# Output stage of a fused top-k attention and two-MoE kernel: raw loads gated two half steps up and no longer chained, and single tiles for gate, value, rounded and rest parts

## The chip, the cores and the metric

The kernel runs on one core of one Trainium2 chip. The metric is the device time of that core for one execution, in microseconds (us). The engines are TensorE (PE in the profile; PEld is its weight loads), VectorE (DVE), ScalarE (ACT), GpSimd (POOL), and SyncE (SP), which issues most of the DMAs. Each engine works through its own instructions in the order in which the program has them.

## The reference, cut to what matters

```python
x = topk_attention(q, k, v)               # batch 4, 8 heads, 576 tokens, head size 64 -> x: [2304, 512]
g = x @ w_gate                            # first MoE, width 1536
x = (g * sigmoid(g)) * (x @ w_val) @ w_out
h = x @ w_in                              # second MoE, width 2048
out = (h * np.cos(h)) @ w_out2            # [2304, 512]
```

All of it is float32. The kernel multiplies in a rounded format by splitting a number into its rounded part and its rest, and takes three products (rounded by rounded, rest by rounded, rounded by rest).

## The kernel before, in words

The program is not written in the order of its instructions. Generators (`gop_proc`, `half_proc`, `join_proc`, `row_proc` and so on) describe chains of steps; each step names an engine, an assumed cost, a due time and whether it starts only when the step before it has ended (the last field, `dep`). A small planner (`Plan.run`, L131) plays these chains against each other: whenever an engine is free in the plan, the ready step with the earliest due time is emitted. `Ring` counts buffers of a tile, and `gate(k)` holds a chain until buffer use k minus n is released; `Event` holds a chain until something is done. The planner's times decide only the order of the instructions on each engine. On the chip an instruction waits for its data and for its buffer, and for everything ahead of it on its engine.

A DMA step has an assumed cost of 1.2 and a latency of 2.0 in the plan (L96). With `dep` true, a chain's next load is ready only when the load before it has landed in the plan.

There are three stages that matter here.

- The attention and the first MoE. For a chunk of up to 256 tokens and 128 columns of the width, ScalarE copies the gate (tile `th`, tanh, and its copy `hg`) and the value (`vv`) out of PSUM, GpSimd multiplies them, ScalarE writes the rounded part and GpSimd the rest into a tile `g` (L859 to L988). `th` with `hg`, and rounded part with rest, each share one tile of [128, 2, 256].
- The hidden stage (`h_proc`, L1403, products at L1417). It multiplies by `w_in` with seven products for each two-by-two block instead of eight (the matrices are first added up into seven combinations), for 4 column blocks of 576 tokens and 16 pairs of rows: h. `cosine` (L1555) turns h into h cos h with a chain ACT, DVE, ACT, ACT, DVE (L1565, L1573, L1578, L1581, L1582) with 2 buffers `k` and 4 buffers `r`; `row_proc` stores the rows to `gd` in HBM (L1598). Every fourth row of the width is stored without the cosine, but for the first 512 tokens; its cosine is taken late, in the output stage. The turns of `cosine` follow one another in the order of the list `sequence` (L1551).
- The output stage. It has 18 half steps s = 0 to 17 (`HS`, L1614): 9 groups of 256 tokens, each with two halves hh of the width. A half step loads four raw blocks of h cos h from `gd`: A11, A21, A22, A12 (`load`, L1774). VectorE makes four sums of them (S3, S1, S2, S4, L1799). For each of the seven operands in `W_ORDER`, ScalarE writes the rounded part (L1821) and VectorE the rest (L1825) into a tile `gp` with 7 buffers, and TensorE runs 12 matmuls of 128x256 (`product`, L1878). In half steps with hh = 1 of group 2 and later, A22 and A12 go through `cosine` first (`late_proc`). After the second half `join_proc` (L1890) adds the seven results up, 7 VectorE instructions (L1926 to L1944), and stores two rows of output blocks (L1911); their due time puts them ahead of everything else. The weights of the output product are split likewise (`wout2_proc`, L1710 and L1713, 28 tiles), when the hidden stage releases the tiles that they go to. `sums_proc` (L1620, adds at L1657) makes their sums during the hidden stage.

Raw blocks have five buffers for even half steps (the tag `xr`) and five for odd ones (`wr`), so half step s takes the buffers of s-2 (`raw_slot`, L1731). Half step 1 is an exception: its A11 lies in the tile `th` and its A21 and A22 in the two tiles `g`, which the first MoE no longer needs, its A12 in a tile `six`, and S3 in a buffer `r`.

What sets the order of the loads is the head of `gop_proc` and its loop over the loads:

```python
s = step_of[g, hh]
if s:
    yield ev_s3[HS[s - 1]]                 # L1750: S3 of the half step before is made
...
for m, a, b in (("A11", 0, 0), ("A21", 1, 0), ("A22", 1, 1), ("A12", 0, 1)):
    yield ring.gate(i)                     # L1840: the buffer is released
    t = yield "DMA", 1.2, load, due(m) - 8.0, True      # L1841
```

Of the kernel before, what the change touches and what calls it, by code (L numbers as in the profile page):

```python
# [24 lines left out]
DM = H * D  # L25
# [15 lines left out]
CB = S  # L41
# [2 lines left out]
ALONE = 1  # L44
BOTH = 5
LATE = (3,)
GLEAD = 12.0
HALF = S // 2
SCALE = 1.0 / math.sqrt(D)
STEEP = 2.0 ** 96  # L50
# [114 lines left out]
def topk_attention_moe_moe(ctx: ExitStack, tc: tile.TileContext, qT, kT, vP, w1, wo1, w2, out):  # L165
# [667 lines left out]

    G, GT = {}, {}
    r_gv = [Ring(1), Ring(1)]
    r_th, r_vv, r_g, r_yo = Ring(1), Ring(2), Ring(2), Ring(1)
    r_y = [Ring(1) for _ in range(NYB)]
# [17 lines left out]
    TH, VV = {}, {}  # L857

    def wide(tag, n, dt=F32):  # L859
        ring = {"vv": r_vv}.get(tag, r_g)  # L860
        return moe.tile([128, MH], dt, tag=tag, name=tag, bufs=ring.n)[:, :n]

    def gates(n):
        t = moe.tile([128, 2, MH], F32, tag="th", name="th", bufs=r_th.n)
        return [t[:, a, :n] for a in range(2)]

    def gated(dt):
        return moe.tile([128, 2, MH], dt, tag="g", name="g", bufs=r_g.n)

    def gate_proc(k, n, gate, ring, i, due, done):  # L870
        yield r_th.gate(k)

        def evac():
            th, hg = TH[k] = gates(n)
            nc.scalar.activation(th, gate, AF.Tanh, scale=0.5)
            nc.scalar.activation(hg, gate, AF.Copy)  # L876

        end = yield "ACT", 0.13 + 0.00157 * n, evac, due - 10.0, True
        ring.free(i, end, plan)
        done.set(end + plan.LAT["ACT"], plan)  # L880
# [12 lines left out]
    def gemm_proc(c, f):  # L893
        k = K0[c] + f
        due = moe_due(c, f)
        if f:
            yield ev_gemm[c, f - 1]
        yield ev_x[c]
        yield ev_w1[f]
        last = c == NCH - 1  # L900
        if last:
            yield ev_psb
        n = SIZES[c] * 128
        gv, done = {}, [Event(), Event()]

        def part(g, kk):
            xh, xl = XH[c, kk][:, :n], XL[c, kk][:, :n]
            for i, (a, m) in enumerate(((0, xh), (0, xl), (1, xh))):
                nc.tensor.matmul(gv[g], W1[f, kk // 2][:, a, g, kk % 2], m, start=kk == 0 and i == 0,  # L909
                                 stop=kk == KT - 1 and i == 2)  # L910

        rings = []
        for g in range(2):
            if last:
                ring, i = r_o[(2 * f + g) % NLAST], (2 * f + g) // NLAST
                yield ring.gate(i)
                gv[g] = pools["psB"].tile([128, DM], F32, tag=f"o{(2 * f + g) % NLAST}", name="gvl")[:, :n]
            else:
                ring, i = r_gv[g], GV0[c] + f
                yield ring.gate(i)  # L920
                gv[g] = gvt[g][:, :n]
            rings.append((ring, i))
            for kk in range(0, KT, RUN_KK):
                run = range(kk, kk + RUN_KK)
                end = yield ("PE", (0.08 + 0.00117 * n) * RUN_KK,
                             lambda g=g, run=run: [part(g, k2) for k2 in run], due, False)
                if g and f == NF1 - 1:
                    for k2 in run:
                        r_x.free(x_index(c, k2), end, plan)
            if not last:  # L930
                plan.start((gate_proc, val_proc)[g](k, n, gv[g], ring, i, due, done[g]), end + plan.LAT["PE"])
            elif not g:
                plan.start(tanh_proc(k, n, gv[g], due, done[g]), end + plan.LAT["PE"])
        ev_gemm[c, f].set(end, plan)
        if last:
            done[1].set(end + plan.LAT["PE"], plan)
            yield done[0]
            yield done[1]
            yield r_vv.gate(k)
            th = TH.pop(k)  # L940
            if f == NF1 - 1:
                ev_tanh.set(done[0].time, plan)

            def silu():
                VV[k] = wide("vv", n)
                nc.vector.scalar_tensor_tensor(VV[k], th, 1.0, gv[0], op0=OP.add, op1=OP.mult)

            def product():
                nc.vector.scalar_tensor_tensor(VV[k], VV[k], 0.5, gv[1], op0=OP.mult, op1=OP.mult)

            end = yield "DVE", 0.36, silu, due - 80.0, True
            rings[0][0].free(rings[0][1], end, plan)
            r_th.free(k, end, plan)
            end = yield "DVE", 0.36, product, due - 80.0, True
            rings[1][0].free(rings[1][1], end, plan)
            vv = VV[k]
        else:
            for g in range(2):
                yield done[g]
            th, hg, vv = TH.pop(k) + VV.pop(k)  # L960
            mul = 0.05 + 0.0026 * n
            yield ("POOL", 0.05 + 0.00135 * n,
                   lambda: nc.gpsimd.tensor_scalar(th, th, 1.0, 0.5, op0=OP.add, op1=OP.mult), due, True)
            yield "POOL", mul, lambda: nc.gpsimd.tensor_mul(th, th, hg), due, True
            end = yield "POOL", mul, lambda: nc.gpsimd.tensor_mul(vv, th, vv), due, True
            r_th.free(k, end, plan)
        yield r_g.gate(G0[c] + f)

        def hi():
            t = gated(F32R)  # L970
            G[c, f] = [t[:, a, :n] for a in range(2)]
            nc.scalar.activation(G[c, f][0], vv, AF.Copy)

        yield "ACT", 0.07 + 0.00092 * n, hi, due, True
        eng, name, cost = (nc.vector, "DVE", 0.33) if last else (nc.gpsimd, "POOL", 0.05 + 0.0025 * n)
        end = yield name, cost, lambda: eng.tensor_sub(G[c, f][1], vv, G[c, f][0]), due - 80.0 * last, True
        r_vv.free(k, end, plan)
        ev_g[c, f].set(end, plan)

    def tanh_proc(k, n, gate, due, done):  # L980
        yield r_th.gate(k)

        def evac():
            TH[k] = gates(n)[0]
            nc.scalar.activation(TH[k], gate, AF.Tanh, scale=0.5)

        end = yield "ACT", 0.27, evac, due - 10.0, True
# [2 lines left out]
    def turned_gemm_proc(c, fp):  # L990
# [27 lines left out]
        gate, val = bank[:, :, 0], bank[:, :, 1]  # L1018

        def evac():  # L1020
            st["th"], st["hg"] = gates(CH)
            st["vv"] = wide("vv", CH)
            nc.scalar.activation(two("th"), gate, AF.Tanh, scale=0.5)
            nc.scalar.activation(two("hg"), gate, AF.Copy)
            nc.scalar.activation(two("vv"), val, AF.Copy)
# [24 lines left out]
        def fetch():  # L1050
            if stored:
                g = xslot[2 + c].rearrange("p a b -> p (a b)")[:, fp * CH:fp * CH + CH]
            else:
                at = c, (fp - NG0) // 2
                if at not in GT:
                    GT[at] = gated(F32)
                g = GT[at][:, fp % 2]
            G[c, fp] = g.rearrange("p (f n) -> p f n", f=2)
            nc.scalar.activation(G[c, fp], st["ps"], AF.Copy)

# [486 lines left out]
    def width_of(n):  # L1547
        j, f = divmod(n, NF2)
        return CB if f % 4 not in LATE else 0 if j else WIDE

    sequence = [n for n in range(NCB * NF2) if width_of(n)] + ["S3"] + [  # L1551
        (g, hh, a) for g in range(WIDE // 256, NGRP) for hh in range(2) if 2 * hh + 1 in LATE for a in range(2)]
    turn_of = {x: i for i, x in enumerate(sequence)}

# [64 lines left out]

    def sums_proc(q):  # L1620
        hh, w = divmod(q, 2)
        due = b_due(3 + 5 * q)
        tiles = {}
        have = {m: Event() for m in ("B11", "B12", "B21", "B22", "T1", "T2", "T3", "T4")}
        used = {m: Event(n) for m, n in (("B11", 1), ("B12", 2), ("B21", 1), ("B22", 2), ("T1", 2), ("T2", 2),
# [105 lines left out]
    def raw_slot(g, hh, m):  # L1731
# [5 lines left out]
            return pb, "xr", r_xr, 6 * NCB + 5 * (s // 2) + k  # L1737
        if s > 1:
            return pb, "wr", r_wr, W2R + NQ2 * SEVEN + 5 * (s // 2 - 1) + k
        g0 = G0[NCH - 1] + NF1  # L1740
        return {"A11": (moe, "th", r_th, K0[NCH]), "A21": (moe, "g", r_g, g0), "A22": (moe, "g", r_g, g0 + 1),
                "A12": (pools["pbx"], "six", r_six, 0), "S3": (pools["pbx"], "r", r_r2, turn_of["S3"])}[m]

    def members(m):
        return slice(m, NF2, 4)

    def gop_proc(g, hh):
        s = step_of[g, hh]
        if s:
            yield ev_s3[HS[s - 1]]  # L1750
        if s == 3:
            yield ev_wt[NQ2 * SEVEN - 1]
        for j in range(g * 256 // CB, (g * 256 + 255) // CB + 1):
# [4 lines left out]
        used = {m: Event(n) for m, n in (("A11", 3), ("A21", 2), ("A22", 2), ("A12", 1), ("S1", 2), ("S2", 2),  # L1758
                                         ("S3", 1), ("S4", 1))}
        home = {"S1": "A21", "S2": "A11", "S4": "A12"}  # L1760

        def due(m):
            return o_due(s * SEVEN + (W_ORDER.index(m) if m in W_ORDER else 2)) - GLEAD

        def alloc(m):
            pool, tag, ring, _ = raw_slot(g, hh, m)
            shape = {"xr": [128, 2, HN], "r": [128, CB], "th": [128, 2, MH], "g": [128, 2, MH]}.get(tag, [128, DM])
            x = pool.tile(shape, F32, tag=tag, name="gr", bufs=ring.n)
            tiles[m] = (x.rearrange("p a b -> p (a b)") if len(shape) == 3 else x)[:, :DM]

        def load(m, a, b):
# [16 lines left out]
        def add(m, x, y, op, wait=()):  # L1788
# [9 lines left out]
                    tiles[m] = tiles[home[m]]  # L1798
                nc.vector.tensor_tensor(tiles[m], tiles[x], tiles[y], op=op)  # L1799

            t = yield "DVE", 0.62, fn, due(m) - 2.0, True
            have[m].set(t, plan)
            done(x, t)
            done(y, t)
            if m == "S3":
                if "S3" in turn_of and s == 1:
                    r_k2.free(turn_of["S3"], t, plan)
                    ev_rows[turn_of["S3"]].set(t, plan)
                ev_s3[g, hh].set(t, plan)
# [18 lines left out]
            ev_gp[g, n, hh].set(t, plan)  # L1828

        def s3():  # L1830
            _, tag, ring, i = raw_slot(g, hh, "S3")
            if tag == "r":
                yield ev_rows[i - 1]
                yield r_k2.gate(i)
            yield ring.gate(i)
            yield from add("S3", "A11", "A21", OP.subtract)

        for m, a, b in (("A11", 0, 0), ("A21", 1, 0), ("A22", 1, 1), ("A12", 0, 1)):
            _, _, ring, i = raw_slot(g, hh, m)
            yield ring.gate(i)  # L1840
            t = yield "DMA", 1.2, lambda m=m, a=a, b=b: load(m, a, b), due(m) - 8.0, True  # L1841
            if b and (g, hh, a) in turn_of:
                plan.start(late_proc(m, a), t)
            else:
# [192 lines left out]
```

## Time and profile before

| | us |
|---|---|
| median of 3 runs | 1257.4 (1253.33 to 1262.25) |
| profiled execution | 1262.9 |
| its span, first to last instruction | 1260.8 |
| TensorE busy | 1172.8 (93%) |
| VectorE busy | 1104.5 (88%) |
| ScalarE busy | 962.8 (76%) |
| GpSimd busy | 575.0 (46%) |

The span is what the trace shows; the execution has 2.1 us around it. In rows of the trace "idle before" is the time in which an engine did nothing just ahead of an instruction, and the name behind the arrow is what ended last of the things that it waited for. `SPq` is the queue of SyncE. A row with a count merges instructions that follow one another; its time runs to the end of the last.

### The profile page before, as it was taken

To read this page: it belongs to the slowest core of one execution; us is meant where nothing else is said; L and a number is where in the kernel's file an instruction comes from. 1 tells how busy PE (TensorE), PEld (TensorE's weight loads), DVE (VectorE), ACT (ScalarE), POOL (GpSimd) and SP (SyncE) were. 2 spreads that over 40 slices of the span, in tenths; PEclk is the share of its full clock that TensorE was granted. 3 is DMA by queue.
4 is the path that set the end of the run, shared out by engine and by line. 5 is a ranking of instruction groups with operands and counts; after the bars stand their busy time and mean duration, and the time that the engine had idled before them with its cause. 6 is when DMAs were issued, how large, how long until landed. Compare 5 with 4: busy or idle time off the path is not lost. (4 is left out here: it accounts for less than half of the span.)

```text
span 1260.8 us, 25036 instructions
## 1 busy us (share of the span) xinstructions
PE 1172.8 (93%) x8368; PEld 1048.2 (83%) x8368; DVE 1104.5 (88%) x2181; ACT 962.8 (76%) x2152; POOL 575.0 (46%) x1036
## 2 busy tenths in 40 slices
PE   6699889999999999999999999999899997889898
PEld 3476647898879998888888988999899997888787
DVE  7999989999999999998999992759988997767776
ACT  4789989888889898898888975549887994434543
POOL 5898966876688767787766655000000000000000
PEclk9899989999999999999999999999999999989999
DMA  7555556665565645566555442753667775434422
GB/s 252 167 167 166 178 161 187 210 214 157 172 186 165 210 157 168 170 183 203 163 183 180 137 129 82 225 158 112 205 208 253 213 235 155 115 96 126 114 84 67
DMA packets 149488, 211.60 MB, mean 168 GB/s; under 512 B 20592, under 2 KB 96880, under 8 KB 149360
## 3 DMA queue, kind: packets, MB, share of 16 engines
q1 hardware_dynamic: 149200, 209.94, 53.6%
q8 instruction: 66, 1.08, 0.4%
q14 instruction: 62, 0.51, 0.1%
q10 hardware_dynamic: 160, 0.07, 0.0%
HBM read 159.62 MB, written 50.33 MB: 167 GB/s over the span
## 5 line engine op out<-in xcount | busy, mean ns | idle before, releaser
L628 DVE MAX8 m<-w 128x8 f32<-128x576 f32 x432 | 309.6, 748 | 1.8
L909 PE MATMUL gv<-x,w 128*128 128x256 f32 x2016 | 271.2, 286 | 0.5 <-ACT th L876 0.5
L909 PEld LDWEIGHTS gv<-x,w 128*128 128x128 f32 x2016 | 252.1, 190 | 3.1 <-ACT th L876 1.3
L1878 PE MATMUL b<-w2o,gp 128*128 128x256 f32 x1512 | 198.8, 292 | 28.1 <-ACT gp L1821 14.5
L1878 PEld LDWEIGHTS b<-w2o,gp 128*128 128x128 f32 x1512 | 190.5, 197 | 36.2 <-DVE gp L1825 19.0
L631 DVE MATCH_REPLACE8 w<-m,w 128x576 f32<-128x576 f32 x288 | 213.2, 743 | 0.0
L1417 PE MATMUL b<-xc,w 128*128 128x288 f32 x1344 | 184.9, 299 | 6.3 <-DVE h L1483 3.2
L1417 PEld LDWEIGHTS b<-xc,w 128*128 128x128 f32 x1344 | 181.6, 190 | 8.5 <-DVE h L1483 4.1
L1080 PE MATMUL y<-wo,g 128*128 128x512 f32 x608 | 170.8, 415 | 9.8 <-POOL wo L249 3.9
L1080 PEld LDWEIGHTS y<-wo,g 128*128 128x128 f32 x608 | 107.1, 189 | 40.9 <-POOL wo L249 5.9
L1821 ACT ACTIVATE gp<-gr 128x512 fp32r<-128x512 f32 x126 | 73.5, 624 | 81.5 <-DVE gr L1799 58.9
L659 ACT ACTIVATE e<-s,b 128x576 f32<-128x576 f32 x144 | 113.5, 789 | 9.5 <-POOL b L642 9.2
L628 DVE MAX8 m<-s 128x8 f32<-128x576 f32 x144 | 107.4, 746 | 14.1 <-ACT s L603 12.4
L670 ACT ACTIVATE e<-e,b 128x576 f32<-128x576 f32 x144 | 114.0, 792 | 4.2 <-POOL b L646 0.3
L603 ACT ACTIVATE s<-sc 128x576 f32<-128x576 f32 x144 | 95.2, 661 | 21.0 <-PE sc L591 15.9
L698 ACT ACTIVATE pt<-tp 128x512 f32<-128x512 f32 (+1 forms) x216 | 101.9, 500 | 10.7 <-PE tp L692 10.2
L631 DVE MATCH_REPLACE8 w<-m,s 128x576 f32<-128x576 f32 x144 | 107.0, 743 | 0.0
L692 PE MATMUL tp<-ident,e 128*128 128x128 f32 x648 | 98.5, 276 | 7.7 <-ACT pt L698 3.5
L598 PE MATMUL sc<-K,q 128*128 128x288 f32 (+1 forms) x512 | 92.3, 307 | 5.8 <-ACT s L603 5.3
L692 PEld LDWEIGHTS tp<-ident,e 128*128 128x128 f32 x648 | 77.8, 141 | 18.8 <-ACT pt L698 6.3
L1825 DVE TENSOR_TENSOR gp<-gr,gp 128x512 fp32r<-128x512 f32 x126 | 83.4, 685 | 5.8 <-ACT gp L1821 5.7
L598 PEld LDWEIGHTS sc<-K,q 128*128 128x128 f32 (+1 forms) x512 | 73.4, 182 | 13.6 <-ACT s L603 8.1
(120 smaller groups left out, 2116.7 us busy)
## 6 DMA issues: line engine op xcount, KB each, us to landing
wo<-wo SPq DMA_DIRECT2D x96, 512.0 KB, 3.7
gr<-gd SPq DMA_DIRECT2D x72, 256.0 KB, 4.6
w_raw<-in_w SPq DMA_DIRECT2D x32, 511.8 KB, 4.3
gd<-r SPq DMA_DIRECT2D x48, 288.0 KB, 2.7
V<-in_vP SPq DMA_DIRECT2D x52, 256.0 KB, 3.0
w<-in_w SPq DMA_DIRECT2D x24, 511.5 KB, 5.8
kx<-in_kT SPq DMA_DIRECT2D x64, 144.0 KB, 3.0
wo<-wo SPq DMA_DIRECT2D x36, 256.0 KB, 3.0
```

What stands on the lines that cost most here:

```text
L598: nc.tensor.matmul(sc[:r1, s, :HALF], q[:, a, (t - t0) * 128:(t - t0) * 128 + r1], k[:, s * HALF:s * HALF + HALF], start=a == 0, stop=a == 1)
L603: nc.scalar.activation(st["s"], sc[:, :, :HALF], AF.Copy)
L628: nc.vector.max(out=st["m"][:, 8 * i:8 * i + 8], in_=st["w"] if i else st["s"])
L631: nc.vector.match_replace(out=st["w"], in_to_replace=st["m"][:, 8 * i:8 * i + 8], in_values=st["w"] if i else st["s"], imm_value=LOWEST)
L659: nc.scalar.activation(st["e"], st["s"], AF.Prelu, bias=st["b"][:, 1:2], scale=SCALE, alpha=STEEP)
L670: nc.scalar.activation(st["e"], st["e"], AF.Exp, bias=st["b"][:, 2:3], scale=1.0, accum_out=smT[c, p, g][:, j:j + 1])
L692: nc.tensor.transpose(st["ps"][:, j - j0], e[:, j * 128:j * 128 + 128], ident)
L698: nc.scalar.activation(pt[:, j0:j1], st["ps"][:, :j1 - j0], AF.Copy)
L909: nc.tensor.matmul(gv[g], W1[f, kk // 2][:, a, g, kk % 2], m, start=kk == 0 and i == 0, stop=kk == KT - 1 and i == 2)
L1080: nc.tensor.matmul(bank, m, w, start=f == 0 and n == 0, stop=f == NF1 - 1 and n == len(terms) - 1)
L1417: nc.tensor.matmul(ps[b], w[:, a, side, kk], x[:, e, kk], start=start and kk == 0 and m == 0, stop=kk == 1 and m == 2, skip_group_check=True)
L1878: nc.tensor.matmul(to, x[:, a, u * 128:u * 128 + 128], y[:, e, u % 2 * QN:u % 2 * QN + QN], start=not hh and n % 2 == 0 and u == 0 and i == 0,
```

## The change

The loads of half step s wait for S3 of half step s-2 instead of s-1, and each load waits for its buffer alone, not for the landing of the load before. Half step 1 takes its raw blocks to other tiles: A11 to a buffer `k`, A21 and A22 to buffers `r`, as S3 did before; for that its loads wait for the last cosine turn of the hidden stage. `th`, `hg`, and the rounded and the rest part of `g` each become a tile of 256 columns; their bytes in all and their numbers of buffers stay. The due times move: operands, loads and sums of the output stage by 2 us (`GLEAD`), A21 by another 1.44 us, S3 to that of A12; `sums_proc` starts at pair 9 and every 4 pairs, where it was pair 3 and every 5. No instruction is added or taken away.

```diff
-GLEAD = 12.0
+GLEAD = 14.0
...
     def wide(tag, n, dt=F32):
-        ring = {"vv": r_vv}.get(tag, r_g)
+        ring = {"th": r_th, "hg": r_th, "vv": r_vv}.get(tag, r_g)
         return moe.tile([128, MH], dt, tag=tag, name=tag, bufs=ring.n)[:, :n]
-
-    def gates(n):
-        t = moe.tile([128, 2, MH], F32, tag="th", name="th", bufs=r_th.n)
-        return [t[:, a, :n] for a in range(2)]
-
-    def gated(dt):
-        return moe.tile([128, 2, MH], dt, tag="g", name="g", bufs=r_g.n)
...
-            th, hg = TH[k] = gates(n)
+            th, hg = wide("th", n), wide("hg", n)
+            TH[k] = [th, hg]
             nc.scalar.activation(th, gate, AF.Tanh, scale=0.5)
             nc.scalar.activation(hg, gate, AF.Copy)
...
-            t = gated(F32R)
-            G[c, f] = [t[:, a, :n] for a in range(2)]
+            G[c, f] = [wide(f"g{a}1", n, F32R) for a in "hl"]
             nc.scalar.activation(G[c, f][0], vv, AF.Copy)
...
-    sequence = [n for n in range(NCB * NF2) if width_of(n)] + ["S3"] + [
+    RAW1 = ("A21", "A22", "S3")
+    sequence = [n for n in range(NCB * NF2) if width_of(n)] + list(RAW1) + [
...
     def sums_proc(q):
         hh, w = divmod(q, 2)
-        due = b_due(3 + 5 * q)
+        due = b_due(9 + 4 * q)
...
-        g0 = G0[NCH - 1] + NF1
-        return {"A11": (moe, "th", r_th, K0[NCH]), "A21": (moe, "g", r_g, g0), "A22": (moe, "g", r_g, g0 + 1),
-                "A12": (pools["pbx"], "six", r_six, 0), "S3": (pools["pbx"], "r", r_r2, turn_of["S3"])}[m]
+        pbx = pools["pbx"]
+        if m == "A11":
+            return pbx, "k", r_k2, turn_of["A21"]
+        if m == "A12":
+            return pbx, "six", r_six, 0
+        return pbx, "r", r_r2, turn_of[m]
...
     def gop_proc(g, hh):
         s = step_of[g, hh]
-        if s:
-            yield ev_s3[HS[s - 1]]
+        if s > 1:
+            yield ev_s3[HS[s - 2]]
+        if s == 1:
+            yield ev_rows[turn_of["A21"] - 1]
...
         def due(m):
-            return o_due(s * SEVEN + (W_ORDER.index(m) if m in W_ORDER else 2)) - GLEAD
+            return o_due(s * SEVEN + AT.get(m, 1)) - GLEAD
...
-            t = yield "DVE", 0.62, fn, due(m) - 2.0, True
+            t = yield "DVE", 0.62, fn, due("A12" if m == "S3" else m) - 2.0, True
...
             if m == "S3":
-                if "S3" in turn_of and s == 1:
+                if s == 1:
+                    r_k2.free(turn_of["A22"], t, plan)
                     r_k2.free(turn_of["S3"], t, plan)
...
         def s3():
-            _, tag, ring, i = raw_slot(g, hh, "S3")
-            if tag == "r":
-                yield ev_rows[i - 1]
-                yield r_k2.gate(i)
+            _, _, ring, i = raw_slot(g, hh, "S3")
             yield ring.gate(i)
             yield from add("S3", "A11", "A21", OP.subtract)
...
             yield ring.gate(i)
-            t = yield "DMA", 1.2, lambda m=m, a=a, b=b: load(m, a, b), due(m) - 8.0, True
+            t = yield "DMA", 1.2, lambda m=m, a=a, b=b: load(m, a, b), due(m) - 8.0, False
```

## Rows read from the trace of the kernel before

**Rows 1.** The page: busy times, granted clock in 40 slices (tenths), one DMA issue.
```profile
PE 1172.8 (93%) x8368; PEld 1048.2 (83%) x8368; DVE 1104.5 (88%) x2181; ACT 962.8 (76%) x2152; POOL 575.0 (46%) x1036
...
PEclk9899989999999999999999999999999999989999
...
gd<-r SPq DMA_DIRECT2D x48, 288.0 KB, 2.7
```

**Rows 2.** The groups by line, TensorE, the matmuls of the output stage.
```profile
L1878 PE MATMUL b<-w2o,gp 128*128 128x256 f32 x1512 | 198.8, 292 | 28.1 <-ACT gp L1821 14.5 <-DVE gp L1825 13.4
```

**Rows 3.** Windows: stage, length, PE, PEld, DVE, ACT, POOL busy, clock, DMA share, GB/s.
```profile
1010.00:1033.60 23.60, 23.60 (x182) 23.60 (x181) 23.60 (x45) 22.94 (x47) 0.00 (x0) 1.00 0.78 240
...
1082.50:1106.10 23.60, 21.34 (x168) 20.33 (x169) 17.83 (x31) 12.40 (x22) 0.00 (x0) 1.00 0.40 113
...
1157.80:1181.50 23.70, 21.01 (x170) 20.15 (x169) 18.60 (x34) 11.87 (x21) 0.00 (x0) 1.00 0.39 112
...
1232.50:1257.40 24.90, 22.46 (x167) 21.59 (x167) 18.28 (x33) 10.83 (x19) 0.00 (x0) 0.93 0.20 60
```

**Rows 4.** Timeline of TensorE, output stage: start, us, instructions, idle before and releaser.
```profile
1033.64 17.32 PE L1878 MATMUL b<-w2o,gp 128*128 128x256 f32 x144
1055.14 0.39 PE L1878 MATMUL b<-w2o,gp 128*128 128x256 f32 x1 [4.18 <-ACT gp L1821]
...
1121.90 11.37 PE L1878 MATMUL b<-w2o,gp 128*128 128x256 f32 x72 [0.88 <-DVE gp L1825]
...
1158.78 1.68 PE L1878 MATMUL b<-w2o,gp 128*128 128x256 f32 x12 [0.18 <-DVE gp L1825]
1160.65 10.20 PE L1878 MATMUL b<-w2o,gp 128*128 128x256 f32 x83 [0.18 <-DVE gp L1825]
1172.29 0.38 PE L1878 MATMUL b<-w2o,gp 128*128 128x256 f32 x1 [1.44 <-ACT gp L1821]
1173.55 8.78 PE L1878 MATMUL b<-w2o,gp 128*128 128x256 f32 x72 [0.88 <-DVE gp L1825]
```

**Rows 5.** Waits of SyncE's queue, 1082 to 1261 us: us in total, times, longest.
```profile
SPq L1911 <- DVE ot L1933: 95.6, 6, 18.3
...
SPq L1774 <- DVE gp L1825: 5.5, 10, 2.0
```

**Rows 6.** Timeline of SyncE, 1100 to 1260 us, around one group's loads.
```profile
1157.55 0.34 SPq L1911 DMA_DIRECT2D out<-ot  x1
1157.98 0.52 SPq L1774 DMA_DIRECT2D gr<-gd  x1
1160.95 0.34 SPq L1911 DMA_DIRECT2D out<-ot  x1
1161.38 4.90 SPq L1774 DMA_DIRECT2D gr<-gd  x7
```

**Rows 7.** The chain that ended last, in order of time: start, us, what.
```profile
1162.71 4.49 DMA gr<-gd
```

**Rows 8.** Timeline of VectorE, 1145 to 1158 us: start, us, instruction, idle before.
```profile
1151.47 1.89 DVE L1825 TENSOR_TENSOR gp<-gr,gp 128x512 fp32r<-128x512 f32 x3
...
1157.10 0.42 DVE L1933 TENSOR_TENSOR ot<-b,ot 128x256 f32<-128x256 f32 x1 [1.96 <-PE b L1878]
1157.44 0.68 DVE L1799 TENSOR_TENSOR gr<-gr 128x512 f32<-128x512 f32 x1
```

**Rows 9.** Timeline of TensorE in the hidden stage, its longest stretch.
```profile
905.64 123.74 PE L1417 MATMUL b<-xc,w 128*128 128x288 f32 x924 [0.55 <-DVE h L1483]
```

**Rows 10.** Line L1657: ns min/median/max, first and last start.
```profile
L1657 DVE TENSOR_TENSOR wr<-wr x16: 679/684/692, 896.0 to 969.7; 128x512 f32<-128x512 f32 x16
```

**Rows 11.** Timeline of VectorE, the last turn of the hidden stage's cosine.
```profile
1037.45 0.75 DVE L1573 SCALAR_TENSOR_TENSOR r<-h,k 128x576 f32<-128x576 f32 x1
```

**Rows 12.** Timeline of SyncE, the last store of the hidden stage.
```profile
1041.91 0.33 SPq L1598 DMA_DIRECT2D gd<-r  x1
```

**Rows 13.** Line L963 (GpSimd on the gate's tanh): idle until, us, times.
```profile
  ACT th L875: 2.6, 4
```

More of the change, by code (lines that the diff above doesn't have):

```diff
@@ L831, in x_proc @@
         ev_x[c].set(end, plan)
-    G, GT = {}, {}
+    G = {}
     r_gv = [Ring(1), Ring(1)]
@@ L983, in evac @@
         def evac():
-            TH[k] = gates(n)[0]
+            TH[k] = wide("th", n)
             nc.scalar.activation(TH[k], gate, AF.Tanh, scale=0.5)
@@ L1020, in evac @@
         def evac():
-            st["th"], st["hg"] = gates(CH)
-            st["vv"] = wide("vv", CH)
+            for name in ("th", "hg", "vv"):
+                st[name] = wide(name, CH)
             nc.scalar.activation(two("th"), gate, AF.Tanh, scale=0.5)
@@ L1053, in fetch @@
             else:
[L1054 to L1057, printed above, removed]
+                g = wide(f"g{'hl'[fp % 2]}1", CH)
             G[c, fp] = g.rearrange("p (f n) -> p f n", f=2)
@@ L1760, in gop_proc @@
         home = {"S1": "A21", "S2": "A11", "S4": "A12"}
+        AT = {m: i for i, m in enumerate(W_ORDER)}
         def due(m):
-            return o_due(s * SEVEN + (W_ORDER.index(m) if m in W_ORDER else 2)) - GLEAD
+            return o_due(s * SEVEN + AT.get(m, 1)) - GLEAD
         def alloc(m):
             pool, tag, ring, _ = raw_slot(g, hh, m)
-            shape = {"xr": [128, 2, HN], "r": [128, CB], "th": [128, 2, MH], "g": [128, 2, MH]}.get(tag, [128, DM])
-            x = pool.tile(shape, F32, tag=tag, name="gr", bufs=ring.n)
+            shape = {"xr": [128, 2, HN], "r": [128, CB], "k": [128, CB]}.get(tag, [128, DM])
+            x = pool.tile(shape, I32 if tag == "k" else F32, tag=tag, name="gr", bufs=ring.n)
+            if tag == "k":
+                x = x.bitcast(F32)
             tiles[m] = (x.rearrange("p a b -> p (a b)") if len(shape) == 3 else x)[:, :DM]
```

## The prediction

> **What bounds the kernel now.** The first view is the page. TensorE is busy 93% of the span and VectorE 88% [rows 1], so the question is where TensorE stands still. The groups by line answer it: ahead of the output stage's matmuls it is idle 28.1 us, nearly evenly behind ScalarE's rounded parts and VectorE's rests [rows 2]. That is a third of all its idle time in the span (1260.8 - 1172.8 = 88 us), and the change is made in this stage, so I read only this stage closely.
>
> The stage's floor comes from an undisturbed stretch: 144 matmuls in 17.32 us [rows 4], the last one's own 0.29 us off [rows 2], is 0.119 us each. A product of 12 takes 1.43 us, a half step of 7 products 10.0, a group of two half steps 20.0 us. What the groups take stands in the timeline and the windows: half step 4 begins at 1082.5 and the last product ends at 1257.4 [rows 3]; 174.9 us for 7 groups, or 25.0 each. A group without a fall of the clock takes 23.7 us (granted clock 1.00) [rows 3]. So each group loses 3.7 us in gaps and after some of them another 1 to 2 us to the clock: where 72 matmuls take 8.78 us at full clock they take 11.37 just after such a gap [rows 4], part of them at 1.2 GHz instead of 2.4.
>
> Next, one group's gaps. TensorE waits 0.18 and 0.18 us around the first product of half step 10 and 1.44 and 0.88 us around the second of half step 11 [rows 4]; the second operand is A12, which in odd half steps is made by the cosine chain. The chain that ended last explains it: the raw load that landed at 1162.71 + 4.49 = 1167.20 [rows 7] is followed by the chain of ACT and DVE until TensorE goes on at 1173.55 [rows 4], 6.3 us later. So the load came too late, and SyncE's timeline tells why: all eight raw loads of a group stand in one burst of 9 us, the first behind one output store, seven behind the next [rows 6]. SyncE's waits give the weight: its queue stood for 95.6 us in 6 waits, up to 18.3 us, at a store that waited for VectorE's L1933 [rows 5], which itself waited for TensorE (idle 1.96 us before it) [rows 8]. While it stood, the loads behind it could have gone: their own waits for a buffer are small, 5.5 us in 10 waits for the largest kind [rows 5]. It is a ring: TensorE's late product, the join, the store, the loads, the cosine, TensorE again.
>
> Why the loads come so late in the queue is in the code. Each half step waits for S3 of the one before, and its four loads wait for one another at 1.2 + 2.0 in the plan, 12.8 us. Two half steps take at least 25.6 us in the plan, against 20.2 for its products at 1.44. The plan itself is bound by its loads.
>
> **The change part by part.** The sum is made against the profiled execution, 1262.9 us; it lies 5.5 above the median of 1257.4.
>
> *Loads two half steps up and unchained (with GLEAD and S3's due).* No instruction is added: the 72 loads stay. In a group's trace the buffers of half step 11 are those of half step 9, whose last rests were written by 1151.47 + 1.89 = 1153.4 [rows 8]; the loads went out at 1158.0 to 1166.3 [rows 6]. They can move up by 5 to 9 us. The wait at the second product was 2.3 us with about 1 us more of clock, so the move covers it. What is late next is VectorE. Its need for a group: 14 rests, 8 sums and 4 instructions of cosine at 0.605 (three rests in 1.89, the last 0.68) are 15.7, and 7 joins at 0.34 (from 1157.10 to 1157.44) are 2.4 [rows 8]; 18.1 us of 20.0, which the windows confirm with 17.8 to 18.6 busy [rows 3]. The hidden stage shows what the planner and the chip do with such a load: TensorE ran 123.74 us without a gap [rows 9], and with VectorE busy 23.6 of 23.6 us at its end [rows 3]. So a group can come near 20.0. I take 20.6: three gaps of 0.18 are left at turns between sums and products. Bounds: 20.0, the floor, and 23.7, what a full-clock group takes now. 7 x (25.0 - 20.6) = 30.8 us gained, between 9 and 35.
>
> *The first four half steps*, 1033.6 to 1082.5, take 48.9 us for 26 products (37.1 at the floor). Here the raws of half steps 2 and 3 come early as well, where a gap of 4.18 us stood in front of half step 2 [rows 4]. But the raws of half step 1 come later than before: its loads now wait for the last turn of the hidden stage's cosine (1037.45 [rows 11]). They would land 4.5 us later [rows 7], at 1042, and with a rounded part and a rest (some 1.4 us) reach TensorE at 1043.4; half step 0 has 5 products left at 1033.6, to 1040.8. That is 2.6 us of wait that before had no counterpart. The weights' splits hold VectorE besides. I take 43 us: 37.1, the 2.6, and 3.3 for VectorE's weights before half step 2; between 40 and 49. 5.9 us gained.
>
> *Sums of w_out2 later.* 16 adds of 0.6 us, at 896 to 970 us now [rows 10]; they move by some 30 us within the hidden stage. Nothing is added; 0, because TensorE has no gap there from 905.64 on [rows 9]. From 2.4 gained (4 adds out of the gaps before 905) to 9.7 lost (all 16 pushed into the last stretch, where VectorE has no free time [rows 3]).
>
> *Single tiles for th, hg, rounded part and rest.* Each instruction reads and writes what it did. A finer tile can take a wait away, not add one: GpSimd waited for the tanh 2.6 us in all, 4 times [rows 13]. 0, at most 2.6 gained. GpSimd at 46% [rows 1] hides the rest.
>
> Sum: 1262.9 - 30.8 - 5.9 = 1226 us. Since groups without gaps should also be without falls of the clock, I take this as the median too and do not subtract from 1257.4.
>
> **The rivals.**
>
> *VectorE's order becomes the bound.* Joins stand ahead of sums and rests in its queue and wait for TensorE: 1.96 us once a group [rows 8]. If only the gap behind the cosine goes (1.44 + 0.88 and its share of the clock), a group falls from 25.0 to about 22.5: 17.5 gained, and 4 at the start: 1241. For it: half of the idle time is behind rests [rows 2]. Against it: in the hidden stage the same kind of queue held no one up [rows 9].
>
> *The loads move in the plan and not on the chip.* They would if the buffers held them or if they still stood behind the stores. The groups stay at 24 to 25 us, the start gains a little: 1256. For it: the five buffers of a half step are unchanged, and the gap is the same in every group. Against it: the loads' own waits are short [rows 5], and the buffers were free 5 us before. The Trainium skill (Perfetto Trace Analysis, Optimization Strategy) reads such a repeating gap on the engine that should be full as a possible sign that there isn't enough on-chip memory for the next tile; by that rule, a change that adds no buffer leaves the gap. The trace agrees about the repetition, not about the buffers.
>
> *Half step 1 pays and nothing is paid back (slower).* S3 of half step 1 takes a buffer r whose row was the last but one or the last to be stored; that store is issued as late as 1041.91 [rows 12] and lands 2.7 us later [rows 1]. The sums S3 and S1 and a split follow, so the third product, due at 1043.7, starts at 1047 to 1048, and the weights' splits queue up behind on VectorE: 4 us, doubled by the queue, and a fall of the clock of 2.6 us (11.37 against 8.78 [rows 4]), 10 us in all. It decides if the seven groups gain under 1.5 us each. With 0.3 each: 1262.9 + 10 - 2 = 1271.
>
> **How the numbers follow.** Forecast 0.55, VectorE's order 0.20, loads not moved 0.15, slower 0.10. The forecast's own range: groups of 20.2 to 21.5 and a start of 40 to 47 give 1220 to 1236; the sums and tiles widen it to 1215 to 1241. For 8 in 10 the range must take in VectorE's order with a few us: 1214 to 1250. About 1% (12.6 us) is what can be told from no change here. Faster by more, below 1244.8: the forecast and most of the second case (0.20), and a sliver of the third: 0.75. Slower by more, above 1270: most of the last, 0.08. The rest, 0.17, is within 1%.
>
> **What would show it.** Right: raw loads spread over a group instead of one burst of eight, SyncE's wait at the stores without loads behind it that TensorE needs; idle time before L1878 down from 28.1 to 8 us or less; windows of a group at 20 to 21.5 us with the clock at 1.00; VectorE at 85 to 90% in the stage. Wrong: TensorE's gaps again behind ScalarE's A12 (the loads did not move), or 1 us and more behind rests in each half step (VectorE's order), or a gap of over 5 us in half step 1 at 1041 to 1048. A hidden stage with new gaps near its end would show the sums to cost.

## The result, and the profile after

The changed kernel takes 1225.61 us (median of 4 runs, 1223.54 to 1231.14) where the kernel before, run beside it and earlier, takes 1259.83 (4 runs): a ratio of 0.974 with a 95% interval of 0.968 to 0.980. The profiled execution took 1231.14 us with a span of 1229.2. The forecast was 1226. The time is met, but in part by luck. The sum started from the profiled execution of 1262.9 us and had a gain of 36.7; from that profile to this one the fall is 31.8. The sum was then taken as the median, which lay 5.5 us below the profiled execution before and lies 5.5 below it now, and this covers the difference.

The page after; the first line answers to the first of [rows 1], the second is the granted clock, and the last two are the groups of the hidden stage's matmuls (now L1407) and of the output stage's (now L1875, to be read against [rows 2]).

```profile
PE 1161.7 (95%) x8368; PEld 1043.1 (85%) x8368; DVE 1103.6 (90%) x2181; ACT 963.7 (78%) x2152; POOL 573.2 (47%) x1036
...
PEclk9899989999999999999999999999989999999999
...
L1407 PE MATMUL b<-xc,w 128*128 128x288 f32 x1344 | 188.3, 301 | 10.1 <-DVE xc L1378 6.3
...
L1875 PE MATMUL b<-w2o,gp 128*128 128x256 f32 x1512 | 181.6, 282 | 3.7 <-DVE gp L1825 3.1
```

Idle time ahead of the output matmuls fell from 28.1 to 3.7 us, and the matmuls themselves from 198.8 busy to 181.6: fewer of them ran at the low clock (granted clock 0.93 in the last group of [rows 3], 1.00 in the first two groups below). The engines' instructions are the same in number. The windows of the changed kernel, same columns as [rows 3]:

```profile
980.00:1010.00 30.00, 26.75 (x187) 26.04 (x186) 26.24 (x47) 24.07 (x47) 0.00 (x0) 0.94 0.68 214
1010.00:1043.70 33.70, 33.70 (x258) 33.70 (x257) 31.75 (x58) 32.12 (x65) 0.00 (x0) 1.00 0.75 231
1043.70:1086.10 42.40, 38.90 (x315) 37.43 (x314) 37.94 (x68) 23.30 (x42) 0.00 (x0) 1.00 0.66 202
1086.10:1106.00 19.90, 19.71 (x167) 19.51 (x166) 17.91 (x33) 11.77 (x21) 0.00 (x0) 1.00 0.45 133
1106.10:1126.00 19.90, 19.90 (x170) 19.90 (x170) 19.47 (x36) 12.73 (x23) 0.00 (x0) 1.00 0.45 133
```

The last two rows are the first two of seven groups: 19.9 us each where [rows 3] has 23.6 to 24.9. The first row is new and speaks against me: the hidden stage now has a stretch with TensorE busy 26.75 of 30 us and a fall of the clock.

TensorE's timeline of the changed kernel, first the gaps in the hidden stage, then the longest stretch of the output stage:

```profile
947.23 43.68 PE L1407 MATMUL b<-xc,w 128*128 128x288 f32 x323 [1.14 <-DVE xc L1378]
991.75 1.19 PE L1407 MATMUL b<-xc,w 128*128 128x288 f32 x7 [0.84 <-DVE h L1473]
993.69 1.06 PE L1407 MATMUL b<-xc,w 128*128 128x288 f32 x6 [0.75 <-DVE xc L1378]
996.42 42.99 PE L1407 MATMUL b<-xc,w 128*128 128x288 f32 x311 [1.67 <-DVE xc L1378]
...
1100.74 125.11 PE L1875 MATMUL b<-w2o,gp 128*128 128x256 f32 x1055 [0.19 <-DVE gp L1825]
```

1055 matmuls without one gap: six of the seven groups run as the hidden stage did in [rows 9]. SyncE's queue shows how. In its timeline the eight loads of the group shown follow one by one over 13.6 us, each when its buffer comes free (compare the bursts in [rows 6]). Its two stores go out together ahead of them; in later groups one or two loads stand between the stores. In the queue's waits (from 1070 us on) the loads now wait for VectorE's rests, that is for their buffers. At the join that held a store for up to 18.3 us [rows 5], now L1930, the longest wait is 5.6 us. One store still waits 16.5 us, in the last group, where no load stands behind it.

```profile
1105.64 3.14 SPq L1908 DMA_DIRECT2D out<-ot  x2
1108.87 13.60 SPq L1773 DMA_DIRECT2D gr<-gd  x8
```

```profile
SPq L1773 <- DVE gp L1825: 53.3, 29, 7.2
SPq L1908 <- DVE ot L1930: 26.5, 7, 5.6
SPq L1908 <- DVE s L1933: 18.5, 2, 16.5
```

Where the time went, by the starts of matmuls in the profiled executions. The first column is the start of the last matmul of the first MoE's gate and value products (L909, now L903; its output products run on for another 4 us); "hidden" runs from there to the start of the last hidden matmul, "first four" from the 25th output matmul (two products run inside the hidden stage) to the 337th, a group is a seventh of the time from there to the last.

| us | first MoE's products end | hidden | first four | a group |
|---|---|---|---|---|
| before | 840.1 | 193.4 | 47.0 | 25.2 |
| after | 842.9 | 200.7 | 42.4 | 19.9 |

From the profile before to the profile after the execution falls by 31.8 us: 7 x 5.3 = 37 in the groups and 4.6 in the first four half steps are gained, 7.3 in the hidden stage and 2.8 ahead of it are lost, and 0.3 is left to rounding. The 37 stands on one profile before; in e3 below, whose edit leaves the output stage alone, a group takes 24.3 us, and with that base it would be some 30.

### The profile page after: what moved, and what is told of

Same layout as the page of the kernel before. It is cut to its first block, busy times and chain, and to the rows that moved or that the text cites. A ratio compares the mean times of both kernels' runs of the same rounds, so it can differ in the third digit from the quotient of the medians.

```text
span 1229.2 us, 25000 instructions
## 1 busy us (share of the span) xinstructions
PE 1161.7 (95%) x8368; PEld 1043.1 (85%) x8368; DVE 1103.6 (90%) x2181; ACT 963.7 (78%) x2152; POOL 573.2 (47%) x1036
## 5 line engine op out<-in xcount | busy, mean ns | idle before, releaser
L903 PE MATMUL gv<-x,w 128*128 128x256 f32 x2016 | 272.5, 286 | 1.5 <-ACT vv L881 1.4
L903 PEld LDWEIGHTS gv<-x,w 128*128 128x128 f32 x2016 | 253.2, 191 | 4.6 <-ACT vv L881 1.6
L1407 PE MATMUL b<-xc,w 128*128 128x288 f32 x1344 | 188.3, 301 | 10.1 <-DVE xc L1378 6.3
L1407 PEld LDWEIGHTS b<-xc,w 128*128 128x128 f32 x1344 | 184.6, 192 | 12.8 <-DVE xc L1378 7.5
L1875 PE MATMUL b<-w2o,gp 128*128 128x256 f32 x1512 | 181.6, 282 | 3.7 <-DVE gp L1825 3.1
L1875 PEld LDWEIGHTS b<-w2o,gp 128*128 128x128 f32 x1512 | 179.7, 188 | 5.4 <-DVE gp L1825 4.3
L1070 PE MATMUL y<-wo,gh 128*128 128x512 f32 x400 | 147.2, 414 | 6.0 <-DMA wo<-wo 5.2
L603 ACT ACTIVATE s<-sc 128x576 f32<-128x576 f32 x144 | 95.2, 661 | 19.9 <-PE sc L591 16.2
L1070 PEld LDWEIGHTS y<-wo,gh 128*128 128x128 f32 x400 | 75.0, 189 | 28.0 <-issue 6.1
L692 PEld LDWEIGHTS tp<-ident,e 128*128 128x128 f32 x648 | 78.9, 143 | 18.1 <-ACT pt L698 5.5
L1070 PE MATMUL y<-wo,gl 128*128 128x512 f32 x208 | 86.2, 421 | 4.0 <-POOL wo L249 3.2
```

Of the source, the lines that this page charges most:

```text
L603: nc.scalar.activation(st["s"], sc[:, :, :HALF], AF.Copy)
L692: nc.tensor.transpose(st["ps"][:, j - j0], e[:, j * 128:j * 128 + 128], ident)
L1070: nc.tensor.matmul(bank, m, w, start=f == 0 and n == 0, stop=f == NF1 - 1 and n == len(terms) - 1)
L1407: nc.tensor.matmul(ps[b], w[:, a, side, kk], x[:, e, kk], start=start and kk == 0 and m == 0, stop=kk == 1 and m == 2, skip_group_check=True)
L1875: nc.tensor.matmul(to, x[:, a, u * 128:u * 128 + 128], y[:, e, u % 2 * QN:u % 2 * QN + QN], start=not hh and n % 2 == 0 and u == 0 and i == 0,
```

## The experiments

All ratios are against the kernel before, run beside it on the same chip. Two questions were open: which edit brings the output stage's gain (and whether it was the ring through SyncE's queue), and what delayed the hidden stage.

**The sums of w_out2.** The changed kernel with the old due times of the sums, and the kernel before with the new ones:

```diff
 # e1, on the kernel after
-        due = b_due(9 + 4 * q)
+        due = b_due(3 + 5 * q)
 # e3, on the kernel before
-        due = b_due(3 + 5 * q)
+        due = b_due(9 + 4 * q)
```

> The changed kernel with the old due times of the sums of w_out2 alone (pair 3 and every 5). Theory: their late place costs the hidden stage about 7 us, because the last four adds stand among the splits of the last column block; without it the last matmul of the hidden stage starts some 7 us earlier than the 1043.5 of the changed kernel's profile, the gaps between 947 and 1002 us are gone, and the time is about 1218 us against 1225. Rival: the hidden stage is later for another reason (the raws of half step 1 that moved, or the order of loads as a whole), and the sums have nothing to do with it: 1225 us, the same gaps.

> The kernel before with the late due times of the sums of w_out2 alone. Theory: 5 to 7 us slower by gaps in the hidden stage, 1266 us. Rival: no change, 1260 us, since VectorE has free time where they go.

Measured: e1 1219.95 us, ratio 0.971 (0.969 to 0.974); e3 1260.25 us, ratio 1.0038 (1.0020 to 1.0056), which is 2.5 to 7 us slower. Against the changed kernel's ratio e1's interval overlaps, so the totals alone don't part them; TensorE's timelines do. In e1 the gaps are gone; in e3, which has nothing else of the change, they are there at the same place of the stage and of the same length as after the change:

```profile
903.03 123.76 PE L1407 MATMUL b<-xc,w 128*128 128x288 f32 x924 [0.55 <-DVE h L1473]
```

```profile
942.47 43.33 PE L1417 MATMUL b<-xc,w 128*128 128x288 f32 x323 [1.19 <-DVE xc L1388]
986.69 1.19 PE L1417 MATMUL b<-xc,w 128*128 128x288 f32 x7 [0.88 <-DVE h L1483]
988.62 1.06 PE L1417 MATMUL b<-xc,w 128*128 128x288 f32 x6 [0.75 <-DVE xc L1388]
991.36 43.00 PE L1417 MATMUL b<-xc,w 128*128 128x288 f32 x311 [1.68 <-DVE xc L1388]
```

VectorE's timeline of the changed kernel shows the collision. The last four adds (L1648) fall between 987.7 and 992.3, among the splits of the last column block (L1378) for which TensorE waits:

```profile
987.74 0.68 DVE L1648 TENSOR_TENSOR wr<-wr 128x512 f32<-128x512 f32 x1
989.01 1.29 DVE L1648 TENSOR_TENSOR wr<-wr 128x512 f32<-128x512 f32 x2
...
991.61 0.68 DVE L1648 TENSOR_TENSOR wr<-wr 128x512 f32<-128x512 f32 x1
992.88 0.75 DVE L1378 TENSOR_TENSOR xc<-xr,xc 128x576 fp32r<-128x576 f32 x1
```

So the theory holds, with 6 us in the hidden stage (199.2 in e3 against 193.4 before; 194.6 in e1 against 200.7 after) where 5 to 7 were expected; in the ten profiles with the early sums the stage lies between 193.0 and 194.8. Some half of the loss is idle time and the rest slower matmuls. The hidden stage's group on the page before, against the one after (188.3 busy, 10.1 idle):

```profile
L1417 PE MATMUL b<-xc,w 128*128 128x288 f32 x1344 | 184.9, 299 | 6.3 <-DVE h L1483 3.2
```

**The two edits of the loads, together and each alone.**

```diff
 # e2: both; e5: the gate alone; e6: the load alone; all on the kernel before
-        if s:
-            yield ev_s3[HS[s - 1]]
+        if s > 1:
+            yield ev_s3[HS[s - 2]]
...
-            t = yield "DMA", 1.2, lambda m=m, a=a, b=b: load(m, a, b), due(m) - 8.0, True
+            t = yield "DMA", 1.2, lambda m=m, a=a, b=b: load(m, a, b), due(m) - 8.0, False
```

> The kernel before with the new gate (S3 two half steps up) and the unchained loads alone; tiles, raws of half step 1, sums and due times as before. Theory: these two edits carry the gain of the output stage; the groups fall from 25.0 to 20.0 to 20.6 us, the first four half steps to 40 to 43, the hidden stage stays; 1260 - 33 - 7 = about 1220 us or a little below. Rival: the earlier due times (GLEAD, S3) are needed as well, since VectorE's order otherwise holds the sums behind the joins: groups at 22.5, 1240 us.

> The kernel before with the gate alone: S3 two half steps up, loads still chained. Theory (the plan was bound by its loads: 12.8 us and one S3 a half step, one half step after the other): two chains now run side by side in the plan, so 12.8 us a half step hide behind 20.2 us a group, and the loads go early on the chip too; groups of 20 to 20.5 us, about 1218 us, like both edits together (1215). Rival: the chain holds the loads of one half step apart whatever the gate is; half the gain stays away, 1235 us.

> The kernel before with the loads unchained alone, the gate still at S3 of the half step before. Theory: a half step's loads take 4.8 + 2 us in the plan instead of 12.8, 15 us a group with S3, under the 20.2 of its products; the plan is no longer bound by its loads and most of the gain is there, 1220 us. Rival: loads that may begin only after the S3 of the half step before are late for the cosine in the odd half steps; groups of 22 to 23 us, 1238 us.

| | us | ratio, interval | first four | a group |
|---|---|---|---|---|
| e2, both | 1215.08 | 0.968 (0.965 to 0.971) | 41.1 | 19.9 |
| e5, gate alone | 1230.78 | 0.979 (0.976 to 0.982) | 42.3 | 21.7 |
| e6, unchained alone | 1218.41 | 0.968 (0.965 to 0.972) | 39.2 | 20.4 |

The two edits of the loads carry the whole gain of the output stage; the earlier due times are not needed for it. The unchaining alone brings nearly all of it, and each loosens the same limit, so their gains don't add up. For e5 neither theory had the number: groups at 21.7, not 20 and not halfway. The chain that ended last, in order of time, shows what held it, and it is still the ring: TensorE's matmuls, a join behind them in VectorE's queue, the store that waits for this join, the load behind the store, its landing, and by the cosine back to TensorE.

```profile
1110.37 5.95 PE b L1878 x47
...
1119.23 0.34 DVE ot L1944
...
1119.59 0.34 SPq L1911
...
1120.02 0.52 SPq L1774
...
1120.60 3.76 DMA gr<-gd
...
1131.98 5.95 PE b L1878 x47
```

Store and load follow each other like this on the chain of five groups of e5. In TensorE's timeline of e6 the stretch from group two on is whole, as after the change:

```profile
1085.90 127.06 PE L1878 MATMUL b<-w2o,gp 128*128 128x256 f32 x1067 [0.30 <-DVE gp L1825]
```

**The stores out of SyncE's queue.** This tests the ring by itself, on the kernel before, with the plan's order untouched.

```diff
-            end = yield "DMA", 1.2, lambda: nc.sync.dma_start(out[256 * g + r * 128:256 * g + r * 128 + 128],
+            end = yield "DMA", 1.2, lambda: nc.gpsimd.dma_start(out[256 * g + r * 128:256 * g + r * 128 + 128],
```

> The kernel before with the two output stores of a group issued by GpSimd, which is idle in this stage, instead of SyncE; the planned order of everything is the same. Theory of the ring (raw loads stand in SyncE's queue behind a store that waits for TensorE): the loads go out 5 to 9 us earlier without any other change, the gaps behind A12 go, groups of 21 to 22.5 us, 1260 - 20 = 1240 us. Rival (the queue only hides it; the order of VectorE and the buffers hold the loads): groups stay at 24 to 25 us, 1258 us.

Measured: 1244.48 us, ratio 0.991 (0.989 to 0.994), groups of 22.9, between the 21 to 22.5 of the theory and the 24 to 25 of the rival. The ring through the stores is real, but less than half of a group's loss: 25.2 to 22.9, of 5.3 to be had (24.3 to 22.9 with e3 as the base). The rest is not the stores: in the timeline of TensorE the gap in front of A12 shrinks from 1.44 and 0.88 us [rows 4] to 0.99 and 0.34 and stays, and SyncE's waits are now nearly all at the loads, for VectorE's rests (the buffers).

```profile
1161.01 0.39 PE L1878 MATMUL b<-w2o,gp 128*128 128x256 f32 x1 [0.99 <-ACT gp L1821]
1161.74 8.78 PE L1878 MATMUL b<-w2o,gp 128*128 128x256 f32 x72 [0.34 <-DVE gp L1825]
```

```profile
SPq L1774 <- DVE gp L1825: 112.0, 42, 8.7
```

Nor is it late loads. In the kernel before, the first step of the cosine (L1565) waited for a raw block in six groups (1106 to 1257 us); in e4 (1100 to 1236 us) no such wait is listed. There ScalarE waits six times at L1920 instead, the copy of a group's first product with which a join begins:

```profile
ACT k L1565 <- DMA gr<-gd: 18.3, 6, 3.7
```

```profile
ACT s L1920 <- PE b L1878: 9.4, 6, 1.6
```

ScalarE's timeline of e4 shows that the copy, which needs TensorE, stands right ahead of the rounding of A12, for which TensorE then waits (the gap of 0.99 above); both cosines had ended by 1159.2.

```profile
1160.06 0.38 ACT L1920 ACTIVATE s<-b 128x256 f32<-128x256 f32 x1 [1.57 <-PE b L1878]
1160.34 1.14 ACT L1821 ACTIVATE gp<-gr 128x512 fp32r<-128x512 f32 x2
```

So what remains in e4 is the planned order. On TensorE, VectorE and ScalarE it is, instruction by instruction, that of the kernel before; in e2 the same copy stands three to six roundings later, and e10 below, which has the stores on GpSimd too but the looser plan, takes 19.9 us a group. The place of this one copy was not changed by itself.

**Single tiles, with the raws of half step 1 in k and r.** The changed kernel with the old gate, chain, due times and sums.

```diff
 # e7, on the kernel after
-GLEAD = 14.0
+GLEAD = 12.0
-        due = b_due(9 + 4 * q)
+        due = b_due(3 + 5 * q)
-        if s > 1:
-            yield ev_s3[HS[s - 2]]
+        if s:
+            yield ev_s3[HS[s - 1]]
...
-            t = yield "DMA", 1.2, lambda m=m, a=a, b=b: load(m, a, b), due(m) - 8.0, False
+            t = yield "DMA", 1.2, lambda m=m, a=a, b=b: load(m, a, b), due(m) - 8.0, True
```

The due times of A21 and S3 are the old ones too.

> The kernel before with single tiles for gate, copy, rounded part and rest, and the raws of half step 1 in the buffers k and r (they can no longer lie in the two-part tiles); gate, chain, due times and sums as before. Theory: 0 for the tiles and 2 to 4 us lost in the first four half steps because half step 1 is loaded after the last cosine turn: 1256 to 1260 us, hardly to be told from before. Rival: the finer tiles take waits away in the first MoE, up to 2.6 us gained.

Measured: 1261.35 us, ratio 1.0035 (1.0014 to 1.0055), 1.8 to 6.9 us slower. e7 has the tiles and the moved raws together; the price stands in the output stage, where only the raws differ. It is above the 2 to 4 us expected: the first four half steps take 52.7 us against 47.0. In TensorE's timeline of e7 half step 1 begins with the longest gap of any run; ScalarE's timeline says why: the operand's rounding stands behind two weight splits that wait for their loads.

```profile
1046.29 0.58 PE L1875 MATMUL b<-w2o,gp 128*128 128x256 f32 x1 [9.02 <-ACT gp L1821]
```

```profile
1044.38 1.34 ACT L1701 ACTIVATE w2o<-wr 128x512 fp32r<-128x512 f32 x2 [3.69 <-DMA wr<-w2d]
1045.62 1.14 ACT L1821 ACTIVATE gp<-gr 128x512 fp32r<-128x512 f32 x2
```

**Due times, gate and stores on top of e2.** e8 adds the earlier due times, e9 takes the S3 gate out of e8 altogether, e10 puts e8's stores on GpSimd.

```diff
 # e8, on e2
-GLEAD = 12.0
+GLEAD = 14.0
-            return o_due(s * SEVEN + (W_ORDER.index(m) if m in W_ORDER else 2)) - GLEAD
+            return o_due(s * SEVEN + (W_ORDER.index(m) if m in W_ORDER else 1)) - GLEAD
-            t = yield "DVE", 0.62, fn, due(m) - 2.0, True
+            t = yield "DVE", 0.62, fn, due("A12" if m == "S3" else m) - 2.0, True
 # e9, on e8
-        if s > 1:
-            yield ev_s3[HS[s - 2]]
 # e10, on e8: the edit of e4
```

> The kernel before with the two edits of the loads, and the earlier due times of the output stage (GLEAD 14, A21 and S3 earlier); tiles, raws of half step 1 and sums as before. Theory: the plan has slack once its loads do not bind, so the due times change nothing: 1215 us as with the two edits alone. Rival: an earlier S3 on VectorE costs or gains in the first four half steps, where VectorE is the bound: 3 us or more either way.

> The kernel of e8 (both edits of the loads, earlier due times) without any gate at an S3; each load waits for its buffer alone. Theory: two half steps up the gate is never what a load waits for last, since five buffers already tie half step s to s-2; groups of 19.9 us and 1215 us as in e8. Rival: without the gate loads of a later half step push into the queue ahead of those that are needed; 1220 us or more.

> The kernel of e8 with the output stores issued by GpSimd. Theory: TensorE is now the bound of the groups (19.9 us against a floor of 20.0 worked out before), so freeing SyncE's queue, worth 12 us in the kernel before (e4), is worth nothing here: 1215 us. Rival: the stores still cost something at the queue, 1210 us or less.

| | us | ratio, interval | first four | a group |
|---|---|---|---|---|
| e8 | 1214.98 | 0.966 (0.964 to 0.969) | 38.5 | 19.9 |
| e9 | 1215.76 | 0.968 (0.965 to 0.972) | 38.5 | 19.9 |
| e10 | 1216.28 | 0.969 (0.966 to 0.972) | 38.5 | 19.9 |

In the output stage the three are alike to a tenth of a microsecond. Two half steps up, the gate never binds the plan: e9's trace has the instructions of e8 in the same order on every engine and in SyncE's queue, so it is the same work for the chip. The stores' queue, worth some 11 us in the kernel before (8 to 14 by e4's interval), is worth nothing once the loads come early: a wait has a price only where something behind it is late. The due times take 2.6 us off the first four half steps (41.1 to 38.5), which the totals (intervals of e2 and e8 overlap) can't confirm. In e8's timeline the stage is two gaps away from its floor:

```profile
1026.24 27.26 PE L1878 MATMUL b<-w2o,gp 128*128 128x256 f32 x229
1054.84 24.41 PE L1878 MATMUL b<-w2o,gp 128*128 128x256 f32 x204 [1.34 <-DVE gp L1825]
1079.43 125.11 PE L1878 MATMUL b<-w2o,gp 128*128 128x256 f32 x1055 [0.18 <-DVE gp L1825]
```

e8 is the best version found: the loads and the due times of the change, without its tiles, its place for the raws of half step 1 and its sums. It stands at 1215 us against 1225.6; the intervals of the two ratios just touch (0.969 and 0.968), and the stages part them: hidden 193.0 against 200.7, output from the 25th matmul on 178.0 against 181.9.

## Why the prediction was right, and where its sum was off

**What bound the kernel.** Right. The plan, bound by its chained loads, put them late; in SyncE's queue they then stood behind stores that wait for TensorE. e6 shows the first (unchaining alone: 1218 us), e4 the second (stores away: some 11 us), and in e5 the chain still runs through the store. I had told it as one ring; the runs show two layers: the queue, up to 2.4 of the 5.3 us of a group, and for the rest the order that the plan had drawn with loads of 25.6 us a group.

**The groups.** Mechanism right, the term mis-sized: 20.6 forecast, 19.9 measured, 35 gained by the windows (from 25.0) instead of 30.8. I kept three gaps of 0.18 a group that did not stay. (From e3's 24.3 a group the gain would be some 30, so the 4 us are not sure.) VectorE's need of 18.1 us was a little low, and so was the 85 to 90% named for it: it is busy 17.9 and 19.5 of 19.9 us in the two groups' windows above, with TensorE never waiting for long. The fall of the clock went with the gaps, as expected: granted clock 1.00 in both windows.

**The base.** I took the sum, made from a profiled execution, as the median too, because groups without gaps should be without falls of the clock. That reason did not hold: the profile after lies 5.5 us above its median, as the one before did. It hid that the sum had 5 us too much gain, and that was luck.

**VectorE's order as the next bound** (the rival at 1241). It did not become one, in any run with both edits. What held e5's groups was the store's ring. What held e4's, by its trace, was ScalarE's order, which no rival had named.

**The first four half steps.** 43 forecast, 42.4 measured. But the price of the later raws of half step 1, put at 2.6 us there, is 5.7 in e7 (52.7 against 47.0) and 5.4 with the new loads (43.9 in e1 against 38.5 in e8). The place was right, and the engine only in part. I named VectorE's weight splits. In e7 it is ScalarE's, waiting for their loads, ahead of the operand. In the changed kernel itself the chain that ended last runs through VectorE: an add (L1798) waits for the store of a row to land, as the slower rival had it, and weight splits (L1704) follow until TensorE goes on.

```profile
1048.53 4.41 DMA gd<-r
...
1053.06 0.06 DVE gr L1798
...
1056.16 0.60 DVE w2o L1704
1056.76 0.62 DVE gp L1825
...
1057.42 15.78 PE b L1875 x131
```

That the early raws of half steps 2 and 3 gained more made up for it.

**The sums of w_out2.** This step failed: "0, because TensorE has no gap there from 905.64 on". A stretch without gaps means only that the work on VectorE fitted in its order so far; it does not say that other work can be put into it. The cost is 6 us of the hidden stage, inside the bounds that I had stated (2.4 gained to 9.7 lost), but I took 0. I looked for the danger in the last stretch, at 1010 to 1033, and it came earlier: at 947, and at 987 to 996, where the last column block is split.

**Single tiles.** 0 taken, and no gain seen: GpSimd's wait for the tanh was 2.6 us in 4 times [rows 13] and is 2.7 us in 4 times after. Their cost is the raws that had to move. The 2.8 us by which the first MoE's products ended later (842.9) are not theirs either: e1 and e7, which have the same tiles, reach that point at 836.3 and 835.1, and without them it lies between 833.1 and 841.9 (e2 to e6 and e8 to e10, which have the program of before up to there).

**The slower rival** (half step 1 pays, nothing is paid back) named a real price, 2 to 7 us when it stands alone (e7), but not the outcome, because seven groups paid 35 back.

**The rule of the Trainium skill** (Perfetto Trace Analysis, Optimization Strategy: a repeating gap can mean too little memory for the next tile). The trace doesn't bear it out here: in e2, with every buffer as before, the idle time ahead of the output matmuls fell from 28.1 to 1.7 us. What remains true in it is that after the change the loads do wait for their buffers (53.3 us in all), but early enough.

## What to carry to other kernels

When the order of instructions comes from a plan, work out the plan's own period for the stage: if its assumed costs make it longer than the work of the busiest engine, the order that it draws can hold the chip even where the data come in time (22.9 us a group in e4, 19.9 in e10). Look also for a transfer that stands in a queue behind one that waits for the engine you want to feed. And a stretch in which an engine never waits is no proof of room: before moving work into it, look which instructions there have a reader waiting.

## What the runs showed that I had not expected

- Unchaining the loads alone gave almost everything (1218.4 us), the wider gate alone some 60% of it (1230.8), and with the loads unchained and the earlier due times the gate could be left out (1215.8).
- The first MoE's gate and value products, the same program up to there in nine of the profiles (before, e2 to e6 and e8 to e10), ended between 833.1 and 841.9 us, and e8 and e9, with the same order of instructions, have spans of 1208.1 and 1218.2. So single times of this kernel move by 9 or 10 us without any change; a difference of 5 us between two versions is settled by the stages of their profiles sooner than by their totals.
